# Attention ahead of two feed-forward layers: unscaled weights, sums carried along the row by TensorE, low halves on GpSimd, two more banks for scores

## The chip, the cores and the metric

The kernel runs on one core of one Trainium2 chip. The metric is device time in microseconds (us), the median of the runs shown. TensorE multiplies matrices (PE in the rows; PEld is its weight load), VectorE is DVE, ScalarE is ACT, GpSimd is POOL, and SyncE (SP) issues nearly all DMAs. Every engine works through its own list of instructions in order, so an instruction that waits holds up all that stand behind it on its engine.

## The reference, cut to what matters

```python
# q, k, v: (4, 12, 448, 64)
q_n, k_n = rmsnorm(q, g_q), rmsnorm(k, g_k)
scores = (q_n @ k_n.T) / sqrt(64)
scores = scores - max(scores, axis=-1)
attn = exp(scores)
attn = attn / (sum(attn, axis=-1) + 1e-9)
x = (attn @ v)                      # laid out as (1792, 768)
h = x @ w_in                        # 768 -> 2048
g = where(h > 0, h, exp(min(h, 0)) - 1)
x = g @ w_out                       # 2048 -> 768
# then: router x @ w_gate, greedy assignment of 1792 tokens to 8 experts
# (224 each), relu(x @ w1[e]) @ w2[e] on each expert's rows
```

The four lines from `scores` to `x`, and the low half of `g`, are what the change touches.

## The kernel before, in words

Numbers that need more than fp16 are kept as two fp16 halves, high and low, and a product takes three matmuls (high by high, low by high, high by low).

Attention walks over 4 batches of 6 pairs of heads. A pair has 448 query rows, in three blocks of 128 rows for both heads (`j` = 0 to 2) and one tail block (`j` = 3) in which the 64 last rows of both heads share a tile. For each block: `scores(j)` makes the products (six matmuls of 448 columns for two tiles `ps`), VectorE takes the row maximum (L533), ScalarE the exponential with its row sum (L535, `accum_out`). `weights(j)` adds 1e-9 (L540) and takes the reciprocal (L541) on VectorE, and GpSimd multiplies each row of the weights by it (L545; L543 also copies the tail rows of the second head to a place of their own). `turn_p(j)` transposes the scaled weights on TensorE (`pta`, `ptb`), and ScalarE (L559) and VectorE (L560) copy them to `PT`. After the four blocks `values` multiplies `PT` with v into `po`; ScalarE makes the high half of the result (L578), VectorE the low half (L579). Row sums lie along the partitions before the transposition; after it the query rows lie along the free dimension.

While batch b is in attention, the first feed-forward product of batch b-1 (`hidden`) runs between: 16 blocks f of 18 matmuls `ph`, then ScalarE and VectorE make `elu_g` (L682 to L685), ScalarE its high half `gt` (L687), VectorE the low half (L688), and SP stores both halves to DRAM (L689, L690). A ring of 6 buffers holds `gt`. The weights come in as pairs of 32-bit words that VectorE turns to fp32 in three instructions (L374, L377, L378), ScalarE scales and rounds them, GpSimd makes the low half (L382): `w_in` during batches 0 and 1, `w_out` during batches 1 and 2. There `w_out` is also transposed by DMA (`wt`) and multiplied with the gate (`gate_product`).

A table of steps (96 for a batch, 16 for a pair) sets what is written when: `scores(j)` at step 4j, `weights(j)` at 4j+1, `turn_p(j)` at 4j+5, `values` at 19, and the tile framework reorders instructions of an engine by its own simulated times. PSUM has 8 banks: 3 for scores (`psS`), 3 for transposes, values, gate and logits (`psT`), 2 for the first product (`psM`), which has nothing to do until batch 0 is through attention.

Stages by the trace, in us of the span: batch 0 from 27 to 140, batch 1 with the first product of batch 0 to 284, batch 2 to 422, batch 3 to 540, the first product of batch 3 to about 617. Then the second product with the routing, then the experts; the change touches nothing there.

## Time and profile before

| what | us |
|---|---|
| median of 3 runs (1158.93 to 1169.1) | 1161.26 |
| the profiled execution | 1164.11 |
| its span (first to last instruction) | 1162.4 |
| PE busy in the span | 1039.3 |
| DVE busy | 784.2 |
| ACT busy | 539.2 |
| POOL busy | 353.9 |

The share of busy time is an average over stages with different limits, so it is read by stage. A wait row names who waited for whom, with the total, the number of times and the longest. Mean durations of instructions on VectorE and GpSimd contain the time in which one held up the other.

### The profile page before, as it was taken

Reading aid. Unit: us, or ns where it says so; the run is one execution under the profiler, and the core shown is the slowest. Engines: PE = TensorE matmul, PEld = TensorE weight load, DVE = VectorE, ACT = ScalarE, POOL = GpSimd, SP = SyncE. Lnnn points to the kernel's source line nnn. Section 1 sums busy time; section 2 is a strip of 40 time slices with the busy share of each in tenths; the row PEclk is TensorE's granted clock in tenths of the full one; section 3 lists DMA queues with packets and bytes.
Section 4 is the critical chain, followed back from the end, with each engine's and each line's share of the span. In section 5 each row is a group of like instructions: output and inputs, shape, how many; then the busy total and the mean of one; then the engine's idle time right before and its main releaser. Section 6 shows DMA issues by size and latency. Waiting matters only on the chain.

```text
span 1162.4 us, 19353 instructions
## 1 busy us (share of the span) xinstructions
PE 1039.3 (89%) x7030; PEld 608.4 (52%) x7030; DVE 784.2 (67%) x1567; ACT 539.2 (46%) x1099; POOL 353.9 (30%) x462
## 2 busy tenths in 40 slices
PE   0687879897989999999999699999999898999997
PEld 0233334343444445444444345555546687888885
DVE  3788898999988775554337777877775565556520
ACT  2676677776777664554430410011102455555520
POOL 3687775757746451220000000000000412222100
PEclk9888889998999989999999899999999899999999
DMA  6355575569997825336823641030003778778710
GB/s 172 78 133 132 147 207 151 145 178 255 245 256 195 194 68 121 81 95 225 328 55 113 194 167 50 21 130 21 22 21 101 239 236 263 223 244 258 237 47 24
DMA packets 190319, 176.48 MB, mean 152 GB/s; under 512 B 114704, under 2 KB 161808, under 8 KB 189456
## 3 DMA queue, kind: packets, MB, share of 16 engines
q1 hardware_dynamic: 186064, 163.78, 49.5%
q0 software_dynamic: 3328, 11.01, 3.0%
q8 instruction: 55, 0.90, 0.3%
q10 hardware_dynamic: 832, 0.46, 0.1%
q14 instruction: 40, 0.33, 0.1%
HBM read 125.92 MB, written 31.98 MB: 136 GB/s over the span
## 4 chain that ended last, share of the span: by engine, by line
PE 48%; DVE 16%; DMA 13%; issue 10%; ACT 6%; POOL 4%; SPq 2%; POOLq 0%; DVEq 0%; ACTq 0%
PE py L324 17%; PE ph L324 12%; DMA st<-in_moe_w_dram 7%; PE po L324 4%; PE pye L324 3%; PE phe L324 3%; PE ps L324 3%; PE rt_pc L324 2%; DVE w L351 2%; DVE sm L533 2%; ACT w L350 2%; DVE cv L377 2%; PE pta L324 2%; DMA qn<-in_q_dram 2%; PE pl L324 1%
## 5 line engine op out<-in xcount | busy, mean ns | idle before, releaser
L324 PE MATMUL ph<-xT,w_in 128*128 128x448 f16 x1152 | 246.1, 358 | 8.2 <-DVE elu_g L685 5.2
L324 PE MATMUL py<-w_out,g 128*128 128x384 f16 x1152 | 204.5, 329 | 0.0
L324 PEld LDWEIGHTS <-w_in 128*128 128x128 f16 x1152 | 107.7, 99 | 127.7 <-issue 46.1
L351 DVE SCALAR_TENSOR_TENSOR w<-st,w 128x768 f16<-128x768 f32 (+1 forms) x112 | 119.2, 1072 | 76.7 <-ACT w L350 71.5
L545 POOL TENSOR_SCALAR pe<-pe,sm 128x448 f32<-128x448 f32 x168 | 126.7, 764 | 138.8 <-DVE sm L541 70.3
L324 PEld LDWEIGHTS <-g 128*128 128x128 f16 x1152 | 107.4, 98 | 89.3 <-issue 26.7
L324 PE MATMUL ps<-kT,qT 64*128 64x448 f16 (+1 forms) x576 | 97.0, 392 | 56.2 <-ACT pe L535 30.7
L350 ACT ACTIVATE w<-st 128x768 f16<-128x768 f32 (+1 forms) x112 | 103.6, 933 | 90.8 <-DMA st<-in_moe_w_dram 86.5
L535 ACT ACTIVATE pe<-ps,sm 128x448 f32<-128x448 f32 x168 | 105.9, 634 | 50.0 <-DVE sm L533 47.4
L324 PE MATMUL pye<-w,hT 128*112 128x512 f16 (+1 forms) x768 | 126.4, 326 | 0.0
L324 PEld LDWEIGHTS <-w 128*128 128x128 f16 x1152 | 111.8, 100 | 3.3 <-DVE xTe L917 1.2
L127 DVE TENSOR_SCALAR rt_C<-rt_row,rt_m 128x1792 f16<-128x1792 f32 x98 | 107.2, 1149 | 8.2 <-PE rt_pc L324 7.4
L324 PE MATMUL phe<-xTe,w 128*128 128x224 f16 x1080 | 111.4, 264 | 1.1 <-DVE xTe L917 1.1
L533 DVE TENSOR_REDUCE sm<-ps 128x1 f32<-128x448 f32 x168 | 100.2, 615 | 17.2 <-PE ps L324 15.2
L324 PEld LDWEIGHTS <-hT 128*112 128x112 f16 x768 | 91.6, 130 | 32.2
L815 ACT ACTIVATE xh<-py 128x384 f16<-128x384 f32 x28 | 13.7, 491 | 175.0 <-PE py L324 158.1
L324 PEld LDWEIGHTS <-qT 64*128 64x128 f16 (+1 forms) x576 | 27.7, 102 | 99.9 <-issue 66.7
L324 PE MATMUL pta<-id,pe 128*128 128x128 f32 x384 | 64.4, 289 | 15.1 <-POOL pe L545 5.8
L967 POOL DMA_INDIRECT out_dram<-yo,idx x16 | 19.5, 1220 | 179.6 <-DVE yo L966 178.0
L685 DVE SCALAR_TENSOR_TENSOR elu_g<-ph,elu_e 128x448 f32<-128x448 f32 x64 | 39.6, 619 | 48.3 <-ACT elu_e L683 48.1
L324 PEld LDWEIGHTS pta<-id,pe 128*128 128x128 f32 x384 | 45.2, 146 | 44.3 <-POOL pe L545 14.7
L201 POOL MEMSET rt_c<- 128x8 f16 x8 | 0.9, 123 | 220.7 <-DVE rt_c L207 216.6
(176 smaller groups left out, 1470.0 us busy)
## 6 DMA issues: line engine op xcount, KB each, us to landing
st<-in_moe_w_dram SPq DMA_DIRECT2D x48, 512.0 KB
st<-in_moe_w_dram SPq DMA_DIRECT2D x64, 384.0 KB
st<-in_moe_w_in_dram SPq DMA_DIRECT2D x24, 512.0 KB
g_d<-gt SPq DMA_DIRECT2D x64, 192.0 KB
g<-g_d SPq DMA_DIRECT2D x16, 768.0 KB
st<-in_moe_w_out_dram SPq DMA_DIRECT2D x16, 512.0 KB
gl<-g_d SPq DMA_DIRECT2D x32, 192.0 KB
wo_d<-wo SPq DMA_DIRECT2D x16, 384.0 KB
```

The costliest lines, as they stand in the source:

```text
L127: i = DVE.tensor_scalar(C.rearrange("p c t -> p (c t)"), row, m[:, s:s + 1], None, op0=ALU.is_le)
L201: nc.gpsimd.memset(c[:, 0:1, :], 0.0)
L324: i = PE_mm(o, l, r, **kw)
L350: ACT.activation(hi, st, AF.Copy, scale=SW)
L351: DVE.scalar_tensor_tensor(lo, st, SW, hi, op0=ALU.mult, op1=ALU.subtract)
L377: DVE.scalar_tensor_tensor(cv, st[:, :, 1], -0x40000000, cv, op0=ALU.bitwise_and, op1=ALU.bitwise_or)
L533: i = DVE.tensor_reduce(out=st[:, 0, u:u + 1], in_=ps[u], axis=AX.X, op=ALU.max, negate=True)
L535: ACT.activation(p[:, u, :], ps[u], AF.Exp, bias=st[:, 0, u:u + 1], accum_out=st[:, 1, u:u + 1])
L545: POOL.tensor_scalar(p[:, u, :], p[:, u, :], st[:, 2, u:u + 1], 1.0, op0=ALU.mult, op1=ALU.mult)
L685: DVE.scalar_tensor_tensor(gf, ph, -SG / SH, e, op0=ALU.mult, op1=ALU.min)
L815: ACT.activation(xh[:, 0], py, AF.Copy, scale=-SX2 / (SG * SW))
L967: st = POOL.indirect_dma_start(out=out, out_offset=bass.IndirectOffsetOnAxis(ap=idx[:, 1, 2 * e + hh:2 * e + hh + 1], axis=0), in_=yo, in_ ...
```

## The change

The weights are no longer scaled. `weights` is gone; a new `tail` keeps only the copy of the tail rows (GpSimd, 64 columns). The sums of all seven tiles of a pair stand in one tile `st`, and a new `sums`, written at step 15, makes all seven reciprocals (with the scale of the result in them) by one addition and one reciprocal on VectorE, splits them into two fp16 halves by two small GpSimd instructions, and has TensorE multiply the halves, broadcast over 64 columns, with the identity: 16 small matmuls bring the reciprocals from the partitions to the free dimension, in a bank of `psT`. ScalarE copies that to `x32`. `values` then multiplies `po` by it on VectorE, ScalarE rounds the high half, VectorE subtracts for the low half.

In `hidden` the low half of `gt` moves from VectorE to GpSimd. For the first five pairs, two of each five score tiles are in the banks `psM`. Some buffers are cut to make room: `ln`, `y2`, `wgt` to one, `wt` from three to two.

```diff
+        def bank(s):
+            s.nb = getattr(s, "nb", 0) + 1
+            if s.n < NP - 1 and s.nb % 5 in (1, 3):
+                return psM.tile([P, S], F32, tag="pm", name="psm")
+            return psS.tile([P, S], F32, tag="ps", name="ps")
...
-        def weights(s, j):
-            p, st = s.P[j]
-            w = 2 if j < NJ else 1
-            DVE.tensor_scalar(st[:, 2, 0:w], st[:, 1, 0:w], 1e-9, None, op0=ALU.add)
-            DVE.reciprocal(st[:, 2, 0:w], st[:, 2, 0:w])
-            if j == NJ:
-                POOL.tensor_scalar(p[:, 1, 0:TAIL], p[:, 0, MAIN:], st[:, 2, 0:1], 1.0, op0=ALU.mult, op1=ALU.mult)
-            for u in range(w):
-                POOL.tensor_scalar(p[:, u, :], p[:, u, :], st[:, 2, u:u + 1], 1.0, op0=ALU.mult, op1=ALU.mult)
+        def tail(s):
+            p = s.P[NJ]
+            POOL.tensor_scalar(p[:, 1, 0:TAIL], p[:, 0, MAIN:], 1.0, 1.0, op0=ALU.mult, op1=ALU.mult)
...
+        def sums(s):
+            iv = s.st[:, 2]
+            DVE.tensor_scalar(iv, s.st[:, 1], 1e-9, 1.0 / SX, op0=ALU.add, op1=ALU.mult)
+            DVE.reciprocal(iv, iv)
+            i16 = att.tile([P, 2, 2 * NJ + 1], F16, name="i16")
+            POOL.tensor_scalar(i16[:, 0], iv, 1.0, 1.0, op0=ALU.mult, op1=ALU.mult)
+            POOL.tensor_sub(i16[:, 1], iv, i16[:, 0])
+            pr = psT.tile([P, S], F32, tag="pt", name="pr")
+            kk = key()
+            for j in range(NJ + 1):
+                for z in range(2):
+                    for u in range(2):
...
+                        mm(pr[r, j * P:min(S, (j + 1) * P)], l, i, key=kk, start=(z == 0), stop=(z == 1),
+                           skip_group_check=True)
+            s.x = att.tile([P, S], F32, name="x32", bufs=1)
+            ACT.copy(s.x, pr)
...
-            ACT.activation(hi, po, AF.Copy, scale=SX)
-            DVE.scalar_tensor_tensor(lo, po, SX, hi, op0=ALU.mult, op1=ALU.subtract)
+            DVE.tensor_mul(s.x, po, s.x)
+            ACT.copy(hi, s.x)
+            DVE.tensor_sub(lo, s.x, hi)
...
-            DVE.tensor_sub(gt[:, 1], gf, gt[:, 0])
+            POOL.tensor_sub(gt[:, 1], gf, gt[:, 0])
...
-                    at(t + 4 * j + 1, p.weights, j)
                     at(t + 4 * j + 5, p.turn_p, j)
+                at(t + 4 * NJ + 1, p.tail)
+                at(t + 4 * NJ + 3, p.sums)
```

VectorE early in batch 1, where the first product begins; before (`sm` are the row statistics, `h` the halves of q and k, `cv` the converted weights, `gt` the halves of the first product):

```order
L378 SCALAR_TENSOR_TENSOR cv<-st,cv 128x512
L540 TENSOR_SCALAR sm<-sm 128x2
L541 RECIPROCAL sm<-sm 128x2
L481 TENSOR_TENSOR h_1815<-kn,h_1815 128x896
L374 TENSOR_SCALAR cv<-st 128x512
L688 TENSOR_TENSOR gt<-elu_g,gt 128x448
L377 SCALAR_TENSOR_TENSOR cv<-st,cv 128x512
L540 TENSOR_SCALAR sm<-sm 128x2
```

and of the change, at about the same place (`x` is the pair's result, `xT` its halves):

```order
L603 TENSOR_TENSOR x_1400<-po,x_1400 128x448
L378 SCALAR_TENSOR_TENSOR cv<-st,cv 128x512
L377 SCALAR_TENSOR_TENSOR cv<-st,cv 128x512
L564 COPY PT<-ptb 128x3x128
L574 TENSOR_SCALAR sm<-sm 128x7
L452 TENSOR_REDUCE ss<-sq 128x14
L378 SCALAR_TENSOR_TENSOR cv<-st,cv 128x512
L575 RECIPROCAL sm<-sm 128x7
L605 TENSOR_TENSOR xT<-x_1400,xT 128x448
```

The pairs of small instructions for each block are now one pair for each two heads, with other work between its two; `gt` is gone from VectorE, and the low half of the pair's result has become a multiplication and a subtraction.

GpSimd in the same stretch, before (`pe` are the weights, `w_in` the low half of the weights):

```order
L474 TENSOR_TENSOR qn<-qn,rs 128x896
L545 TENSOR_SCALAR pe<-pe,sm 128x448
L382 TENSOR_TENSOR w_in_133<-cv,w_in_133 128x512 x2
L545 TENSOR_SCALAR pe<-pe,sm 128x448 x4
L382 TENSOR_TENSOR w_in_133<-cv,w_in_133 128x512 x2
L494 TENSOR_SCALAR kT<-kT 128x2x64 x2
L545 TENSOR_SCALAR pe<-pe,sm 128x448 x2
```

and of the change (`i` are the halves of the reciprocals):

```order
L714 TENSOR_TENSOR gt<-elu_g,gt 128x448
L494 TENSOR_SCALAR kT<-kT 128x2x64 x2
L549 TENSOR_SCALAR pe<-pe 128x64
L454 TENSOR_TENSOR qn<-qn,gain 128x896
L382 TENSOR_TENSOR w_in_133<-cv,w_in_133 128x512
L714 TENSOR_TENSOR gt<-elu_g,gt 128x448
L577 TENSOR_SCALAR i_1641<-sm 128x7
L382 TENSOR_TENSOR w_in_134<-cv,w_in_134 128x512
L578 TENSOR_TENSOR i_1641<-sm,i_1641 128x7
```

The scalings of `pe` are gone, `gt` has come, and the two small instructions on the reciprocals stand among the long ones. On TensorE, in a pair of batch 1, the end of the new matmuls `pr` (16 with a weight load each) stands ahead of the pair's last transposition:

```order
L324 LDWEIGHTS i_1380
L324 MATMUL pr<-id_60,i_1380 64x64
L324 MATMUL pta<-id_65,pe 128x128 x4
L324 LDWEIGHTS w_in_133
L324 MATMUL ph<-xT,w_in_133 128x448
```

So TensorE, which takes its list in order, comes to `pr` before it can transpose the tail block or go on with the first product.

## Rows read from the trace of the kernel before

**Rows 1.** Busy time by engine, granted clock, DMA share and GB/s, by stage.

```profile
27.00:140.00 113.00, 85.58 (x443) 37.89 (x441) 93.37 (x186) 74.31 (x179) 81.52 (x101) 0.86 0.49 119
140.00:284.00 144.00, 122.93 (x712) 57.99 (x710) 133.38 (x259) 107.11 (x245) 99.66 (x115) 0.95 0.71 186
284.00:422.00 138.00, 124.96 (x809) 62.70 (x805) 118.09 (x290) 97.75 (x241) 79.65 (x101) 0.94 0.80 199
422.00:540.00 118.00, 118.00 (x719) 56.85 (x719) 68.16 (x167) 65.12 (x154) 25.86 (x42) 1.00 0.43 103
540.00:617.00 77.00, 75.47 (x401) 36.04 (x399) 23.49 (x43) 28.45 (x50) 3.47 (x24) 1.00 0.58 212
```

**Rows 2.** Waits in batch 0: who for whom, us in total, times, longest.

```profile
PE ps L324 <- ACT pe L535: 14.9, 15, 2.8
PEld pta L324 <- POOL pe L545: 11.1, 11, 3.8
DVE ss L452 <- ACT sq L451: 8.4, 6, 2.2
```

**Rows 3.** VectorE, addition to the sums (L540), by stage: stretch, us, busy (times).

```profile
27.00:140.00 113.00, 10.99 (x28) 0.86 0.49 119
140.00:284.00 144.00, 5.49 (x24) 0.95 0.71 186
284.00:422.00 138.00, 6.00 (x24) 0.94 0.80 199
```

**Rows 4.** VectorE, reciprocals (L541), by stage.

```profile
27.00:140.00 113.00, 4.00 (x26) 0.86 0.49 119
140.00:284.00 144.00, 3.96 (x26) 0.95 0.71 186
284.00:422.00 138.00, 3.70 (x24) 0.94 0.80 199
```

**Rows 5.** VectorE, low half of the first product (L688), by stage.

```profile
140.00:284.00 144.00, 13.05 (x16) 0.95 0.71 186
284.00:422.00 138.00, 12.16 (x16) 0.94 0.80 199
422.00:540.00 118.00, 10.38 (x16) 1.00 0.43 103
```

**Rows 6.** L688 alone: ns minimum/median/maximum, first and last start.

```profile
L688 DVE TENSOR_TENSOR gt<-elu_g,gt x64: 598/624/2060, 152.0 to 611.4; 128x448 f16<-128x448 f32 x64
```

**Rows 7.** Groups by line and shape: busy us, mean ns | idle before, what ended it.

```profile
L545 POOL TENSOR_SCALAR pe<-pe,sm 128x448 f32<-128x448 f32 x168 | 126.7, 764 | 138.8 <-DVE sm L541 70.3 <-PE pta L324 18.5 <-ACT cv L380 8.0
L382 POOL TENSOR_TENSOR w_in<-cv,w_in 128x512 f16<-128x512 f32 x24 | 31.2, 1302 | 7.3 <-ACT w_in L381 7.1
L382 POOL TENSOR_TENSOR wo<-cv,wo 128x256 f16<-128x256 f32 x16 | 14.0, 874 | 5.9 <-ACT wo L381 5.9
L465 POOL TENSOR_SCALAR ss<-ss 128x28 f32<-128x28 f32 x12 | 3.4, 286 | 9.5 <-ACT ln L459 9.1
L468 POOL TENSOR_TENSOR y<-y,ss 128x28 f32<-128x28 f32 x12 | 4.6, 383 | 0.6
L541 DVE RECIPROCAL sm<-sm 128x2 f32<-128x2 f32 x72 | 11.4, 159 | 1.0
L579 DVE SCALAR_TENSOR_TENSOR xT<-po,xT 128x448 f16<-128x448 f32 x24 | 14.8, 615 | 11.5 <-ACT xT L578 11.5
L578 ACT ACTIVATE xT<-po 128x448 f16<-128x448 f32 x24 | 12.9, 538 | 15.7 <-PE po L324 15.7
L324 PE MATMUL pte<-id,xg 112*128 112x112 f16 x192 | 14.5, 220 | 9.6 <-DMA xg<-x_d,idx 5.7 <-ACT xTe L917 3.0 <-issue 0.9
L324 PE MATMUL po<-PT,vn 128*64 128x448 f32 x288 | 63.2, 576 | 0.0
L324 PE MATMUL po<-PT,vt 128*128 128x448 f32 x48 | 27.0, 648 | 5.4 <-DVE PT L565 5.3
```

**Rows 8.** The chain that ended last, in batch 2: start, us, what.

```profile
334.39 5.05 DMA wt<-wo
359.09 3.75 DMA wt<-wo
```

More of the change, by code (lines that the diff above doesn't have):

```diff
@@ L456, in rms @@
         def rms(s):
-            ln = att.tile([P, 2, NB2], F32, name="ln")
+            ln = att.tile([P, 2, NB2], F32, name="ln", bufs=1)
             ACT.activation(ln, s.ss, AF.Ln, scale=1.0 / D, bias=eps)
@@ L465, in newton @@
             POOL.tensor_scalar(ss, ss, 1.0 / D, 1e-6, op0=ALU.mult, op1=ALU.add)
-            y2 = att.tile([P, 2, NB2], F32, name="y2")
+            y2 = att.tile([P, 2, NB2], F32, name="y2", bufs=1)
             POOL.tensor_mul(y2, rs, rs)
@@ L509, in scores @@
                 s.PT = att.tile([P, 2 * NJ + 1, S], F32, name="PT")
+                s.st = att.tile([P, 3, 2 * NJ + 1], F32, name="sm")
             w = 2 if j < NJ else 1
@@ L512, in scores @@
             s.P = getattr(s, "P", {})
-            st = att.tile([P, 3, 2], F32, name="sm", bufs=6)
-            s.P[j] = (p, st)
-            ps = [psS.tile([P, S], F32, tag="ps", name="ps") for u in range(w)]
+            st = s.st[:, :, 2 * j:2 * j + w]
+            s.P[j] = p
+            ps = [s.bank() for u in range(w)]
             kk = key()
@@ L535, in scores @@
                 ACT.activation(p[:, u, :], ps[u], AF.Exp, bias=st[:, 0, u:u + 1], accum_out=st[:, 1, u:u + 1])
-        def weights(s, j):
-            p, st = s.P[j]
-            w = 2 if j < NJ else 1
-            DVE.tensor_scalar(st[:, 2, 0:w], st[:, 1, 0:w], 1e-9, None, op0=ALU.add)
-            DVE.reciprocal(st[:, 2, 0:w], st[:, 2, 0:w])
-            if j == NJ:
-                POOL.tensor_scalar(p[:, 1, 0:TAIL], p[:, 0, MAIN:], st[:, 2, 0:1], 1.0, op0=ALU.mult, op1=ALU.mult)
-            for u in range(w):
-                POOL.tensor_scalar(p[:, u, :], p[:, u, :], st[:, 2, u:u + 1], 1.0, op0=ALU.mult, op1=ALU.mult)
+        def tail(s):
+            p = s.P[NJ]
+            POOL.tensor_scalar(p[:, 1, 0:TAIL], p[:, 0, MAIN:], 1.0, 1.0, op0=ALU.mult, op1=ALU.mult)
         def turn_p(s, j):
-            p = s.P.pop(j)[0].rearrange("p u k -> p (u k)")
+            p = s.P.pop(j).rearrange("p u k -> p (u k)")
             ta = psT.tile([P, NJ + 1, P], F32, tag="pt", name="pta")
@@ L565, in turn_p @@
                 DVE.tensor_copy(s.PT[TAIL:, NJ, MAIN:S], ta[TAIL:, NJ, TAIL:])
+        def sums(s):
[10 more added lines that the diff above has]
+                    for u in range(2):
+                        r = slice(u * D, (u + 1) * D)
+                        l, i = (i16[:, z, 2 * j + u:2 * j + u + 1].broadcast_to([P, D]), id16) if j < NJ else \
+                            (i16[r, z, 2 * j:2 * j + 1].broadcast_to([D, D]), id16[r, r])
+                        mm(pr[r, j * P:min(S, (j + 1) * P)], l, i, key=kk, start=(z == 0), stop=(z == 1),
+                           skip_group_check=True)
+            s.x = att.tile([P, S], F32, name="x32", bufs=1)
+            ACT.copy(s.x, pr)
         def values(s):
@@ L612, in gate_products @@
             for z in range(2):
-                wts.append(gat.tile([P, KC, P], F16, name="wt", bufs=3))
+                wts.append(gat.tile([P, KC, P], F16, name="wt"))
                 nc.sync.dma_start_transpose(wts[z], wo[:, z, :])
@@ L625, in gate_product @@
                    stop=(z == 1 and c == KC - 1), skip_group_check=True)
-        t = gat.tile([P, NE], F32, name="wgt")
+        t = gat.tile([P, NE], F32, name="wgt", bufs=1)
         ACT.copy(t, pw[:, NE:])
```

## The prediction

> **What bounds the kernel now.** I read the busy time by stage first, because the change touches only the five stages up to 617 us [rows 1]. In batch 3 (422 to 540) TensorE is busy for all 118.0 of 118 us, VectorE for 68.2: there TensorE is the bound, and time taken from VectorE buys nothing. In batches 1 and 2 VectorE is busy 133.4 of 144 and 118.1 of 138 us (93% and 86%), more than any other engine's useful work: the same attention and the same first product took TensorE 118 us in batch 3, so it could do batches 1 and 2 in about that. In batch 0 VectorE has 93.4 of 113 us, TensorE 85.6 with a mean granted clock of 0.86, that is, a part of the stage at 1.2 instead of 2.4 GHz after it had idled. GpSimd is busy for 81.5, 99.7 and 79.7 us in the first three, ScalarE for 74.3, 107.1 and 97.8: neither is the bound. So batches 0 to 2 go at VectorE's pace, with some latency in batch 0, and batch 3 and the first product of batch 3 (TensorE 75.5 of 77 us) at TensorE's.
>
> Second, the waits in batch 0 [rows 2]: TensorE waits 14.9 us for a bank of scores that ScalarE still reads, and 11.1 us (weight loads) for GpSimd's scaled weights. Third, the work that the change takes from VectorE, by stage [rows 3 to 5].
>
> **The change part by part.** All sums are for one stage of six pairs.
>
> *VectorE, sums.* Additions and reciprocals go: 10.99 + 4.00 = 15.0 us in batch 0, 5.49 + 3.96 = 9.5 in batch 1, 6.00 + 3.70 = 9.7 in batch 2 [rows 3, 4]. One addition and one reciprocal of 7 columns come for each pair. The nearest row is the reciprocal of 2 columns at 159 ns [rows 7]; 2 x 0.16 x 6 = 1.9 us.
>
> *VectorE, result.* Instead of one instruction on PSUM (L579, 615 ns [rows 7]) there are a multiplication that reads PSUM and SBUF, which I price like L579, so that it cancels, and a subtraction in SBUF with the shape of L688. That one takes 598 ns at least, 624 in the middle and up to 2060 [rows 6]; its mean by stage is 12.16/16 = 0.76 to 13.05/16 = 0.82 us beside a busy GpSimd and 10.38/16 = 0.65 in batch 3 [rows 5]. I take 0.72: 6 x 0.72 = 4.3 us (3.6 to 4.9).
>
> *VectorE, first product.* L688 goes: 13.05 us in batch 1, 12.16 in batch 2, 10.38 in batch 3 [rows 5].
>
> VectorE's balance is therefore -15.0 + 1.9 + 4.3 = -8.8 us in batch 0, -9.5 - 13.05 + 6.2 = -16.3 in batch 1, -9.7 - 12.16 + 6.2 = -15.7 in batch 2. Batch 3 and the 77 us behind it save on VectorE too, but TensorE hides that.
>
> *GpSimd.* 168 scalings at 764 ns go, 126.7 us in all [rows 7]. The low half of 448 columns has no row on GpSimd; between 874 ns for 256 and 1302 for 512 columns of the same operation [rows 7] it is 874 + 428 x 192/256 = 1195 ns, 1.2 us. 64 of them are 77 us, 19 in a stage. The two small instructions have 286 and 383 ns as their nearest rows [rows 7], 0.67 x 24 = 16 us. GpSimd is left with 126.7 - 77 - 16 = 34 us less work, and stays under 85 of about 128 us in batch 1. The subtraction takes 1.2 us where VectorE took 0.62, but the first product is 18 matmuls long and six buffers deep, so I cost that at nothing; the stores to DRAM and, from batch 2 on, the logits wait the half microsecond more. If the cover is gone, TensorE waits for a buffer.
>
> The Trainium skill speaks against this part: GPSIMD Engine Reference, section Engine selection, puts elementwise work on VectorE, since GpSimd is about twice as slow for two inputs. The trace agrees (1.2 against 0.62 us). By that rule alone the 64 moved instructions cost 64 x 0.6 = 37 us more than they did; that would be the sum if GpSimd were what everything waits for, and by the rows it isn't.
>
> *ScalarE.* A copy of 448 columns from PSUM for each pair, like L578 at 538 ns [rows 7]: 3.2 us a stage, 110 us in batch 1. That is under VectorE's new 117, but no longer far under.
>
> *TensorE.* 16 matmuls of 128 columns for each pair. The nearest row is the transposition of 112 columns, 192 of them busy for 14.5 us, 75 ns each [rows 7]: 1.2 us for a pair, 7.2 for a stage. The two heads write different halves of the partitions; where the value products do that, 288 of them take 63.2 us, 0.22 each, against 27.0/48 = 0.56 for the ones over all partitions [rows 7], so they run side by side, which would make it 3.6. I take 4 (nearer to the row that has the halves). In batches 0 to 2 this lies in TensorE's idle time (113 - 86, 144 - 123, 138 - 125 us [rows 1]); in batch 3 it adds 4 us.
>
> *TensorE's waits.* The transposition no longer waits for reciprocal and scaling; that is worth something in batch 0 (11.1 us [rows 2]), below nothing elsewhere. The chain now ends in `pr`, and behind `pr` stand the tail's transposition and the first product. Between the last scores of a pair and its `pr` the new order has work of the next pair or of the first product, so I take no wait.
>
> *Banks and buffers.* Two banks more in batch 0 answer the 14.9 us of waits for ScalarE [rows 2]; VectorE's row maxima are as many as before and end the same chain, so I count nothing beyond VectorE's saving, and 14.9 us as the far bound. The fewer buffers for `wt` cost nothing as long as the transposing DMAs come in time. They don't do so by much: in batch 2 the chain goes through them with pieces of 5.05 and 3.75 us [rows 8], with the DMA engines at 0.80 of the stage [rows 1]. 0.80 x 138 = 110 us of transfers would be 0.90 of a stage of 122 us. So of the 15.7 us in batch 2 I count 12.
>
> **Sum.** One microsecond of VectorE is one of the stage in batches 0 and 1: -8.8 - 16.3 - 12 + 4 = -33.1 us. The profiled execution took 1164.1 us (span 1162.4): 1131. The median of the runs is 2.85 us below it, so 1128.
>
> **The rivals.**
>
> *More comes back than VectorE saves.* If the waits were the bound, batch 0 would give 14.9 + 11.1 = 26 us, and batches 1 and 2 would fall to batch 3's 118 us, by 26 and 20: -26 - 26 - 20 + 4 = -68, so 1093. For it speaks that GpSimd leaves the chain from exponential to transposition; against it that VectorE would then have 117 us of work in 118.
>
> *The work hardly gets shorter.* ScalarE at 110 us, TensorE at 118 and DMA at 110 stand close behind VectorE, and in batch 0 VectorE also waits for ScalarE's squares (8.4 us [rows 2]). If only a third of VectorE's 41 us arrives, it is -14 + 4 = -10: 1151, no change by measure (I call within 1%, 1149.6 to 1172.9 us, the same).
>
> *Slower: TensorE waits at every `pr`.* The chain runs from the last row sum over VectorE's two instructions, between which the new order puts a reduction and a conversion, to GpSimd's two, between which stands a 1.3 us low half of the weights. If that comes 3.3 us late for each of 24 pairs, 24 x 3.3 = 79 us are lost, and 1128 + 79 = 1207. It decides from 33/24 = 1.4 us a pair on. For it speaks the order of the rows; against it that the transposition of the old kernel waited for the same chain, and lost 11 us to it in batch 0 only.
>
> *GpSimd holds VectorE up.* The Trainium skill, SBUF — State Buffer, section Who interferes with whom, says that a VectorE instruction with two inputs in SBUF is held by a GpSimd instruction that reads SBUF. The spread of L688 (598 to 2060 ns [rows 6]) agrees. As GpSimd's work falls by 34 us and VectorE loses 64 such instructions for 24 new ones, this leans to the faster side, and has no chance of its own.
>
> **How the numbers follow.** VectorE's saving, 0.50; more, 0.17; a third, 0.20; waits at `pr`, 0.13. The first has 1113 to 1145 as its own range: below it batch 0 with 11 us more and batch 2 with all of its 15.7, above it batches 1 and 2 with half of theirs and 7.2 us for TensorE in batch 3. To leave out 2 in 10, the range starts at 1093, the middle of the second case, holds the third and ends where a wait at `pr` of about 1.3 us for each pair would bring it, at 1160. Faster by over 1% are the first two and a quarter of the third, 0.72; slower a part of the last, 0.10; the same 0.18.
>
> **What would show it.** Batches 0 to 2 shorter by about 9, 16 and 12 us, batch 3 longer by about 4; VectorE's busy time in batch 1 near 117 us; 64 `gt` on GpSimd at about 1.2 us; `pr` matmuls at 75 ns or less with no wait of TensorE before them. It would be wrong if TensorE waits for the halves of the reciprocals, if stores of `gt` stand at the head of SP's list waiting for GpSimd while the loads behind them come late, or if batch 0 is held by its loads.

## The result, and the profile after

The changed kernel takes 1175.67 us (median of 4 runs, 1174.29 to 1178.95) where the kernel before, on the same chip, takes 1162.01: a ratio of 1.0113, 95% interval 1.0072 to 1.0155. It is slower by 1.1%; I had predicted 1128 us and a range up to 1160. The profiled execution has a span of 1173.2 us against 1162.4.

The busy time of the engines on the page after (us, share of the span, instructions):

```profile
PE 1051.0 (90%) x7414; PEld 617.5 (53%) x7414; DVE 748.9 (64%) x1383; ACT 548.6 (47%) x1123; POOL 306.9 (26%) x406
```

Over the whole span VectorE lost 784.2 - 748.9 = 35.3 us of work and GpSimd 353.9 - 306.9 = 47.0. So the change takes work away, and the time does not follow. Where it goes is seen by stage. The view is the same as [rows 1]: stretch, its length, busy time (instructions) of PE, PEld, DVE, ACT, POOL, granted clock, DMA share, GB/s. The bounds are the ends of batch 0 to 3 (the last low half of `xT` in each), then of the first product of batch 3:

```profile
27.00:150.30 123.30, 90.24 (x549) 42.37 (x548) 95.40 (x161) 81.03 (x192) 54.89 (x77) 0.86 0.47 115
150.30:283.60 133.30, 122.35 (x789) 59.14 (x787) 112.23 (x191) 101.20 (x236) 75.47 (x86) 0.99 0.74 184
283.60:431.50 147.90, 131.23 (x924) 65.40 (x924) 123.06 (x260) 105.17 (x259) 72.49 (x92) 0.97 0.82 198
431.50:551.30 119.80, 119.80 (x799) 57.81 (x798) 56.95 (x123) 66.22 (x157) 20.27 (x33) 1.00 0.40 98
551.30:629.00 77.70, 75.02 (x399) 35.96 (x397) 13.88 (x29) 29.17 (x50) 19.94 (x40) 1.00 0.57 212
```

By the same marks, to a tenth, the kernel before took 113.1, 143.8, 138.5, 117.0 and 77.7 us. So batch 0 is longer by 10.2 us, batch 1 shorter by 10.4, batch 2 longer by 9.3, batch 3 longer by 2.8, and what comes behind (routing and experts) shorter by 1.0: together +10.9 of the 10.8 us by which the span grew. Batches 0 and 1 taken together end at the same time as before (283.6 against 283.9).

VectorE's busy time against [rows 1] is 2.0 us more in batch 0, 21.2 less in batch 1 and 5.0 more in batch 2: 14.2 us less over the three, where I had forecast 40.8. A batch ends here with one instruction, and what else has been done by then is not the same in every kernel. Batch 0 holds 11 conversions of weights (L374) and 10 halves of q and k (L481), before the change 10 and 8; batch 1 holds 22 and 4, before 25 and 8. So a part of what batch 0 takes longer and batch 1 shorter is work that moved over the border between them, and the two are better read together.

The operations of the change, by line and shape (columns as in [rows 7]):

```profile
L714 POOL TENSOR_TENSOR gt<-elu_g,gt 128x448 f16<-128x448 f32 x64 | 71.8, 1122 | 163.2 <-ACT gt L713 162.5 <-ACT wgt L653 0.6
L324 PE MATMUL pr<-id,i 128*64 128x128 f16 x288 | 14.0, 231 | 2.4 <-ACT PT L563 1.2 <-POOL i L577 0.9 <-DVE PT L564 0.2
L603 DVE TENSOR_TENSOR x<-po,x 128x448 f32<-128x448 f32 x24 | 14.8, 618 | 30.3 <-PE po L324 30.3
L605 DVE TENSOR_TENSOR xT<-x,xT 128x448 f16<-128x448 f32 x24 | 19.0, 791 | 2.1 <-ACT xT L604 2.0
L590 ACT COPY x<-pr 128x448 f32<-128x448 f32 x24 | 12.7, 531 | 2.3 <-PE pr L324 2.2
L574 DVE TENSOR_SCALAR sm<-sm 128x7 f32<-128x7 f32 x24 | 8.1, 338 | 4.9 <-ACT pe L544 4.8
L575 DVE RECIPROCAL sm<-sm 128x7 f32<-128x7 f32 x24 | 4.7, 197 | 0.4
L324 PEld LDWEIGHTS <-i 128*64 128x64 f16 x288 | 9.7, 113 | 10.6 <-issue 7.0 <-POOL i L577 1.2 <-POOL i L578 1.1
```

The addition took twice its price (338 ns for 159), but no price here is far enough off to be worth more than 3 us a stage. TensorE's matmuls wait 2.4 us before `pr` in the whole span, of them 0.9 for GpSimd's halves, and the weight loads before them 2.3 for the halves: the rival "waits at every `pr`" did not come.

The waits in batch 0 of the kernel after (who for whom, us in total, times, longest), beside [rows 2]:

```profile
PE po L324 <- DVE PT L569: 10.4, 4, 4.3
ACT sq L451 <- DMA kn<-in_k_dram: 9.5, 3, 8.8
DVE ss L452 <- ACT sq L451: 9.4, 4, 5.9
PEld pta L324 <- ACT PT L563: 7.3, 5, 5.4
PE ps L324 <- ACT pe L544: 7.2, 5, 3.6
PEld pta L324 <- ACT pe L544: 5.4, 2, 5.0
```

The wait for a bank of scores has halved (14.9 to 7.2 us), and that of the transposition for GpSimd's scaled weights is gone. In their place the transposition waits for ScalarE, and the values for the copies of the last transposes. ScalarE's wait for the loads of k, 3.8 us in the kernel before, does not explain batch 0, though loads were one of my signs of being wrong: it is 9.6 us in a_noscale_wt3 (below), whose batch 0 takes 113.3 us.

The transposed gate weights, first before, then after: what TensorE idled for before the instructions that read `wt`, and who waited, with us and times (from the view of the tile `wt` between 240 and 440 us, that is, the end of batch 1 and batch 2). Before:

```profile
  DMA wt<-wo: 1.5, 2
  PEld L324: 0.8, 1
  PE pw L324: 0.7, 1
```

After:

```profile
  DMA wt<-wo: 24.0, 24
  PEld L324: 13.3, 12
  PE pw L324: 10.8, 12
```

With two buffers TensorE comes to `wt` too early 12 times and stands for 10.8 us, 8.2 of them in batch 2 (the weight loads count the same waits once more).

### The profile page after: what moved, and what is told of

It is laid out like the page before. It is cut to its first block, busy times and chain, and to the rows that moved or that the text cites. A ratio compares the mean times of both kernels' runs of the same rounds, so it can differ in the third digit from the quotient of the medians.

```text
span 1173.2 us, 19770 instructions
## 1 busy us (share of the span) xinstructions
PE 1051.0 (90%) x7414; PEld 617.5 (53%) x7414; DVE 748.9 (64%) x1383; ACT 548.6 (47%) x1123; POOL 306.9 (26%) x406
## 4 chain that ended last, share of the span: by engine, by line
PE 48%; DVE 16%; DMA 13%; issue 10%; ACT 6%; POOL 3%; SPq 3%; POOLq 0%; DVEq 0%; ACTq 0%
PE py L324 17%; PE ph L324 12%; DMA st<-in_moe_w_dram 8%; PE po L324 3%; PE ps L324 3%; PE pye L324 3%; DVE sm L542 2%; PE rt_pc L324 2%; DVE w L351 2%; PE pta L324 2%; ACT w L350 2%; DVE cv L377 2%; DMA wt<-wo 1%; PE phe L324 1%; PE pl L324 1%
## 5 line engine op out<-in xcount | busy, mean ns | idle before, releaser
L324 PE MATMUL ph<-xT,w_in 128*128 128x448 f16 x1152 | 240.8, 355 | 6.1 <-DVE elu_g L711 4.3
L324 PEld LDWEIGHTS <-w_in 128*128 128x128 f16 x1152 | 106.8, 98 | 119.8 <-issue 35.5
L324 PE MATMUL ps<-kT,qT 64*128 64x448 f16 (+1 forms) x531 | 90.7, 373 | 39.6 <-DMA qT<-h 24.9
L714 POOL TENSOR_TENSOR gt<-elu_g,gt 128x448 f16<-128x448 f32 x64 | 71.8, 1122 | 163.2 <-ACT gt L713 162.5
L544 ACT ACTIVATE pe<-ps,sm 128x448 f32<-128x448 f32 x153 | 96.3, 632 | 31.5 <-DVE sm L542 31.0
L542 DVE TENSOR_REDUCE sm<-ps 128x1 f32<-128x448 f32 x153 | 91.8, 615 | 11.9 <-PE ps L324 5.6
L324 PEld LDWEIGHTS <-qT 64*128 64x128 f16 (+1 forms) x576 | 26.3, 100 | 79.8 <-issue 46.8
L324 PE MATMUL po<-PT,vn 128*64 128x448 f32 x288 | 65.8, 596 | 0.0
```

The source lines that it names most:

```text
L324: i = PE_mm(o, l, r, **kw)
L542: i = DVE.tensor_reduce(out=st[:, 0, u:u + 1], in_=ps[u], axis=AX.X, op=ALU.max, negate=True)
L544: ACT.activation(p[:, u, :], ps[u], AF.Exp, bias=st[:, 0, u:u + 1], accum_out=st[:, 1, u:u + 1])
L714: POOL.tensor_sub(gt[:, 1], gf, gt[:, 0])
```

## The theories, and the lengths by stage

My first theory after the result was: batch 2 is longer because of two `wt` buffers instead of three, and batch 0 because `pr` and its chain stand in the way of something. The rivals: GpSimd's `gt` slows batch 2; VectorE's multiplication and subtraction at the end of each pair slow batch 0; the order that the framework makes by its simulated times is another after any edit, and the stages differ for that alone. The lengths by stage of all kernels that were run, from one profile each (us, batch 0 counted from 27 us), with the ratio of the times and its interval:

| kernel | b0 | b1 | b0 + b1 | b2 | b3 | ratio to before |
|---|---|---|---|---|---|---|
| before | 113.1 | 143.8 | 256.9 | 138.5 | 117.0 | 1 |
| b_wt2 | 112.5 | 142.7 | 255.2 | 149.8 | 116.8 | 1.0094 (1.0065 to 1.0123) |
| b_gate284 | 115.8 | 143.4 | 259.2 | 149.3 | 116.1 | 1.0112 (1.0069 to 1.0155) |
| b_gtpool | 115.1 | 141.0 | 256.1 | 156.6 | 117.0 | 1.0105 (1.0072 to 1.0139) |
| b_gate325 | 113.1 | 140.0 | 253.1 | 137.7 | 123.6 | 0.9971 (0.9954 to 0.9989) |
| b_gtbankgate | 115.8 | 143.5 | 259.3 | 137.3 | 123.6 | 0.999 (0.9968 to 1.0013) |
| after | 123.3 | 133.4 | 256.7 | 147.8 | 119.8 | 1.0113 (1.0072 to 1.0155) |
| a_gtdve | 122.0 | 136.1 | 258.1 | 150.3 | 120.5 | 1.0125 (1.0066 to 1.0184) |
| a_mulpool | 121.3 | 135.8 | 257.1 | 151.2 | 119.7 | 1.0125 (1.0065 to 1.0186) |
| a_nobank | 127.2 | 135.5 | 262.7 | 150.3 | 119.8 | 1.0188 (1.012 to 1.0256) |
| a_wt3cv2 | 123.5 | 136.4 | 259.9 | 149.1 | 119.8 | 1.0101 (1.0058 to 1.0144) |
| a_cv2x2 | 120.8 | 139.2 | 260.0 | 144.6 | 119.8 | 1.009 (1.0066 to 1.0115) |
| a_noscale_wt3 | 113.3 | 128.6 | 241.9 | 155.5 | 117.5 | 0.997 (0.9948 to 0.9992) |
| a_smallonly | 115.7 | 136.8 | 252.5 | 145.7 | 117.3 | 1.0024 (0.9994 to 1.0055) |
| a_sumsnocopy | 121.7 | 127.1 | 248.8 | 150.6 | 123.1 | 1.0028 (1.0004 to 1.0052) |
| a_sumsonly | 125.9 | 135.1 | 261.0 | 145.3 | 124.5 | 1.0104 (1.0065 to 1.0143) |
| a_prpm | 116.6 | 149.7 | 266.3 | 151.4 | 119.8 | 1.0208 (1.0168 to 1.0249) |
| a_prpm0 | 117.0 | 146.9 | 263.9 | 144.8 | 119.8 | 1.0164 (1.0139 to 1.019) |
| a_wt3cv2_gate | 121.4 | 136.0 | 257.4 | 136.5 | 124.3 | 1.004 (1.0013 to 1.0067) |
| a_prpm0_gate | 115.9 | 144.2 | 260.1 | 137.7 | 126.8 | 1.0071 (1.0043 to 1.0099) |

Names with b_ are the kernel before with an edit, with a_ the changed kernel with an edit.

How much a length means can be read from the traces. In before, b_wt2, b_gate284, b_gate325 and b_gtpool every engine has the same instructions in the same order until batch 0 is over, and it took 112.5 to 115.8 us: 3.3 us come without any edit. Nor is the profiled execution always a middle one: that of a_sumsnocopy took 1176.29 us where the median of its runs is 1169.56, those of a_noscale_wt3 and b_gtpool took 4.6 and 4.4 us more than their medians, and that of a_prpm0 6.3 less. The ratios are of the medians.

## Batch 2: the buffers of wt, or the order

**Two buffers alone.**

```diff
-wts.append(gat.tile([P, KC, P], F16, name="wt", bufs=3))
+wts.append(gat.tile([P, KC, P], F16, name="wt"))
```

> The kernel before with one thing of the change alone: two buffers for the transposed w_out (wt) instead of three. Theory 'buffer': the 9 us that batch 2 lost (147.9 against 138.5 us) are TensorE's waits for wt (18 us on its two lists after, 1.5 before), so this alone makes batch 2 longer by 6 to 10 us and the whole 1168 to 1172. Rival 'DMA share': batch 2 is held by the transfers as such, which are the same in both kernels, and the buffer moves nothing: 1162 within 4.

Measured: batch 2 took 149.8 us, 11.3 more than before, and no other batch moved by over 1.1 us. That looked like the whole answer. But TensorE waits for `wt` only 4.4 us there, not 11. In the same view of `wt`, of b_wt2:

```profile
  DMA wt<-wo: 9.8, 12
  PEld L324: 5.4, 6
  PE pw L324: 4.4, 6
```

**Three buffers given back to the changed kernel** (with two instead of three for `cv`, since the memory does not hold both).

```diff
-wts.append(gat.tile([P, KC, P], F16, name="wt"))
+wts.append(gat.tile([P, KC, P], F16, name="wt", bufs=3))
 (and the tag cv: bufs=3 -> bufs=2)
```

> The changed kernel with three buffers for wt again; the room comes from the converted weights (cv), two buffers instead of three. Theory 'buffer': batch 2 falls from 147.8 to 136 to 140 us, and the whole to 1162 to 1167, if the fewer cv buffers cost nothing. Rival 'transfers': batch 2 stays at 146 or more, the whole at 1174 or more.

Batch 2 took 149.1 us: nothing came back, though TensorE's wait for `wt` fell from 10.8 to 4.7 us in the same view. So the third buffer, paid for with one of `cv`, does not bring batch 2 back. A kernel with two `cv` buffers, two for `x32` and still two `wt` took 144.6 there, less than the one with three. Its own question was whether the single buffer of `x32` holds batches 0 and 1; they took 260.0 us against 256.7, so no gain shows:

> The changed kernel with two buffers for x32 instead of one (room again from cv). Theory 'one x32': the copy of a pair's reciprocals waits until the pair before has its low half, and holds a bank of psT meanwhile; with two, batches 0 and 1 together fall by 6 to 15 us from 257, the whole to 1160 to 1170. Rival: that copy has time; within 4 us of the two batches, the whole 1172 to 1180 (batch 2 has still two buffers for wt).

**An edit that takes no work away and adds none.** The kernel before, with the gate's products spread over steps 180 to 284 instead of 280.

```diff
-Spread(gate_products(), NG, 180, 280)
+Spread(gate_products(), NG, 180, 284)
```

> The kernel before with the gate's products spread over steps 180 to 284 instead of 180 to 280, which is next to nothing by itself but moves instructions in the scheduler's order. If batch 2 of the kernel before (138.5 us, where all changed kernels with the old spread have 144 to 157) is a robust result of its three `wt` buffers: batch 2 137 to 140 us and total 1160 to 1165 us. If the order there is fragile and every edit moves it: batch 2 143 to 152 us and total 1167 to 1177 us.

It took 1179.06 us, a ratio of 1.0112 (1.0069 to 1.0155): the same loss as the whole change. Its batch 2 by stage:

```profile
286.30:435.50 149.20, 130.75 (x828) 64.29 (x826) 124.11 (x293) 99.73 (x247) 85.05 (x103) 0.92 0.79 185
```

It has three `wt` buffers, and the view of `wt` shows next to no wait:

```profile
  DMA wt<-wo: 0.5, 2
  PEld L324: 0.3, 1
  PE pw L324: 0.2, 1
```

So batch 2 grows by 10.8 us with three buffers, with the same work in the program, and with next to nothing waiting for `wt`. What differs first is the order that the framework makes: in the two traces every engine has the same instructions in the same order up to 258 us of the span, and behind that it has not. In the longer stage VectorE is then busy for 124.1 us instead of 118.1, GpSimd for 85.1 instead of 79.7, and TensorE's mean granted clock is 0.92 instead of 0.94 [rows 1]. The clock is not what a long batch 2 needs, since the changed kernel has 147.8 us at 0.97. Of the 15 other kernels with a spread to 280 or 284, all have 144 to 157 us in batch 2; the 138.5 of before, on which my sum stood, was the exception. Which instruction's place makes the 11 us I did not find, and it stays open. The single buffers of `ln`, `y2` and `wgt` were given back in no run.

**The gate's products spread further**, into batch 3, in the kernel before and in the changed one (with the three buffers).

```diff
-Spread(gate_products(), NG, 180, 280)
+Spread(gate_products(), NG, 180, 325)
```

> The kernel before with the gate products spread over steps 180 to 325 instead of 180 to 280. If they are what holds batch 2: batch 2 falls from 138.5 to 126 to 131 us, batch 3 rises by 3 to 6, the whole 1155 to 1161. If VectorE's work as such holds batch 2, the same, as VectorE's work moves with them; if neither, within 4 us of 1163.

> As a_wt3cv2, with the gate products (loads, conversion, transposing DMA) spread over steps 180 to 325 instead of 180 to 280, so that a third of them falls into batch 3, where TensorE is the bound and VectorE, ScalarE and the DMA engines have half of their time free. If transfers and conversions hold batch 2, batch 2 falls to 122 to 130 us and batch 3 rises by 0 to 6: the whole 1148 to 1158. Rival 'in-order lists': the work just makes batch 3 longer, and the whole stays within 5 us of a_wt3cv2.

Batch 2 took 137.7 and 136.5 us, and in two more kernels with this spread 137.3 and 137.7: not the 122 to 131 that I expected if the gate's products were what holds it. Batch 3, at TensorE's pace, pays 6.6 us in the kernel before and 4.5 in the changed one (against a_wt3cv2). That is the one setting in which batch 2 had the same length in every kernel tried, four of them. Batch 2 and batch 3 of b_gate325 by stage:

```profile
280.10:417.90 137.80, 124.87 (x780) 61.47 (x779) 119.58 (x272) 99.06 (x240) 81.75 (x101) 0.94 0.81 195
417.90:541.40 123.50, 122.97 (x778) 59.35 (x776) 74.20 (x196) 68.48 (x166) 30.54 (x46) 1.00 0.50 120
```

Under this spread the change (with three `wt` and two `cv`) can be weighed with batch 2 out of the way: 1.004 against 0.9971, that is, 0.7% slower, about 8 us. Those are the 8.3 us of batch 0 (121.4 against 113.1), less 4.0 in batch 1 and 1.2 in batch 2, plus 0.7 in batch 3 and 3.2 behind it: 7.0 us of span. Each of the two kernels is one order of several possible, so a part of this may be the order again.

## Batch 0: what the sums cost

**The whole scaling left out.** No additions, reciprocals, `pr` or multiplication; the values' result is not divided by the row sums. Three `wt` buffers.

```diff
-at(t + 4 * NJ + 3, p.sums)
 (sums removed; values as in the kernel before)
```

> The changed kernel with three buffers for wt and without the scaling by the reciprocals at all: no sums, no pr, no x32, the halves of the result as before the change (so its output lacks the division by the row sums). Theory 'new chain': what VectorE saved in batches 0 and 1 is eaten by the new chain (sums, pr, x32 in one buffer, the multiplication that waits for the values' product); without it batches 0 and 1 together fall from 257 to 228 to 240 us. Rival 'VectorE not the bound': the pairs go at the pace of in-order lists and latencies whatever VectorE has to do; 250 us or more for the two.

Batches 0 and 1 by stage:

```profile
27.00:140.30 113.30, 83.74 (x442) 38.15 (x439) 87.21 (x136) 76.88 (x185) 52.88 (x65) 0.86 0.55 124
140.30:268.90 128.60, 118.26 (x692) 56.79 (x690) 105.60 (x182) 98.00 (x231) 66.38 (x69) 1.00 0.75 187
```

Batch 0 has 113.3 us with VectorE at 87.2 us and GpSimd at 52.9, and had 113.1 with 93.4 and 81.5 [rows 1]: taking VectorE's and GpSimd's scaling away altogether gives nothing there. Batch 1 falls by 15.2, to 128.6, though VectorE's work falls by 27.8; there TensorE's 118.3 is then the most. Together the two take 241.9 us, just above the 228 to 240 of the theory 'new chain' and well under its rival's 250: VectorE has 33.9 us less to do than before, 15.0 of them arrive in the time, and the changed kernel with its chain takes 14.8 again (256.7). This is one kernel in one order, but more than the 4.0 us by which before, b_wt2 and b_gate284 differ over the two batches. In all it came to 0.997, since batch 2 took 17 us more.

**The parts of the sums, one after the other.** From the kernel without scaling to the changed one, each without dividing the result: first the small instructions alone; then the 16 matmuls of each pair; then ScalarE's copy.

```diff
 a_smallonly:  DVE and POOL instructions of sums; pr and ACT.copy(s.x, pr) left out
 a_sumsnocopy: and the 16 matmuls pr
 a_sumsonly:   and ACT.copy(s.x, pr)
```

> The changed kernel with a part of the sums alone: one addition and one reciprocal of 7 columns on VectorE and the two halves of the reciprocals on GpSimd for each pair. The 16 matmuls `pr` on TensorE and the copy of `pr` on ScalarE are left out, and the values' result is not divided by the row sums. Batch 0 (27 us to the end of the 6th low half of xT) took 113.3 us with no sums at all and 125.9 with sums, `pr` and copy. If the small instructions at the end of VectorE's and GpSimd's lists hold batch 0: 121 to 127 us. If `pr` or its copy does it: 112 to 116 us. Total 1163 to 1178 us.

> The same with the 16 matmuls `pr` of each pair, but without ScalarE's copy of them; the values' result is not divided by the row sums. If TensorE's matmuls or the bank that `pr` takes from the three that transpositions and values share hold batch 0: 121 to 127 us against 112 to 116 without them. If ScalarE's copy, which waits for `pr` and stands ahead of exponentials and squares in its list, holds it: 112 to 116 us here as without `pr`. Total 1163 to 1178 us.

> The changed kernel with sums, pr and the copy to x32 as they are, but the result not multiplied by x32 (halves made from the values' product as before the change, so the output lacks the division by the row sums). It splits the 10 us of batch 0 (123.3 with the whole chain, 113.3 without it). Theory 'multiplication': the cost is VectorE's multiplication, which waits for the values' product at the head of its list; batch 0 at 112 to 116, batches 0 and 1 together 240 to 248. Theory 'pr': the cost is pr in TensorE's list and in a bank of psT, with its copy on ScalarE; batch 0 at 119 to 124, the two 250 or more.

Batch 0 of a_smallonly by stage:

```profile
27.00:142.70 115.70, 83.11 (x447) 38.34 (x446) 89.19 (x150) 76.11 (x184) 55.61 (x77) 0.85 0.53 120
```

and of a_sumsnocopy:

```profile
27.00:148.70 121.70, 89.88 (x542) 41.09 (x538) 92.91 (x155) 77.43 (x186) 57.45 (x79) 0.85 0.51 125
```

Batch 0 took 113.3, 115.7, 121.7 and 125.9 us: there the largest step, 6.0 us, comes with the matmuls. But its border moves, and a_sumsnocopy was profiled in a long execution. Batches 0 and 1 together took 241.9, 252.5, 248.8 and 261.0 us. By the medians, on one chip, the last three kernels took 1167.43, 1169.56 and 1179.75 us: the matmuls are worth 2 us there, and 10 come with ScalarE's copy (ratios 1.0028 and 1.0104, with intervals apart). Even that is less than the 1.1% that another order made in b_gate284. So the new chain, with the order that comes with it, costs 14.8 us in the two batches, and which of its links costs them is open. The matmuls' busy time, at least, is small: in the changed kernel they are, by stage and for the tile `pr` alone (PE, then ACT):

```profile
27.00:150.30 123.30, 4.41 (x96) 3.23 (x6) 0.86 0.47 115
150.30:283.60 133.30, 4.22 (x96) 3.20 (x6) 0.99 0.74 184
```

TensorE has 123.3 - 90.2 = 33 us idle in batch 0, room enough for 4.4. The steps of 2.4 and 4.2 us beside it are no larger than what other edits move batch 0 by (112.5 to 115.8 in the kernels without `pr`, 120.8 to 125.9 in those with it in `psT` and with banks for the scores).

**Multiplication and subtraction moved off VectorE** (to GpSimd, by way of a copy on ScalarE):

```diff
-DVE.tensor_mul(s.x, po, s.x)
-DVE.tensor_sub(lo, s.x, hi)
+o = s.PT[:, 0, :]; ACT.copy(o, po)
+POOL.tensor_mul(s.x, o, s.x)
+POOL.tensor_sub(lo, s.x, hi)
```

> The changed kernel, but ScalarE takes the values' result out of PSUM, GpSimd multiplies it with the reciprocals and makes the low half, so that nothing of the result is left on VectorE. Theory 'result on VectorE': VectorE's waits for the product (8.5 us in batch 0) and two instructions of 0.6 us a pair go; batch 0 falls by 6 to 12 us, batch 1 by 2 to 5, the whole to 1155 to 1167. Rival 'banks' or 'loads': batch 0 stays at 120 or more and the whole within 4 us of 1176.

Batch 0 took 121.3 us, batch 1 135.8: VectorE's two instructions at the end of a pair are not what holds batch 0.

**The bank of `pr`.** `pr` takes one of the three banks of `psT` that the transposes and the values go round in. In the changed kernel it was put into one of the two banks of the first product: throughout, and in another kernel for the six pairs of batch 0 alone.

```diff
-pr = psT.tile([P, S], F32, tag="pt", name="pr")
+pr = psM.tile([P, S], F32, tag="pm", name="pr")     # a_prpm
+(the same if s.n < NP, else psT)                    # a_prpm0
```

> The changed kernel, complete, with `pr` in one of the two banks of the first product instead of one of the three that the transpositions, the values and the gate's product share. If it is the missing bank that costs batch 0 its 10 us: batch 0 113 to 117 us, total 1163 to 1169 us. If it is the work itself or its place in the lists: batch 0 121 to 126 us, and batch 1 and 2 longer by the first product's wait for banks, total 1174 to 1182 us.

> The changed kernel with `pr` in a bank of the first product for the six pairs of batch 0 alone, where the first product doesn't run yet; from batch 1 on it lies where the change put it. With `pr` there throughout, batch 0 came down from 123.3 to 116.6 us and batch 1 rose from 133.4 to 149.7. If the bank is what costs batch 0 most: batch 0 115 to 118 us, batch 1 132 to 137, batch 2 anywhere from 144 to 152 (the old spread of the gate's products), total 1166 to 1176 us. If batch 0 gained from another order and not from the bank: batch 0 121 to 126 us, total 1173 to 1183.

Batch 0 fell by 6.7 and 6.3 us, to 116.6 and 117.0, and by 5.5 in a third kernel with it (a_prpm0_gate against a_wt3cv2_gate), as I expected if the missing bank costs it. But the three kernels have one and the same order of instructions until batch 0 is over, and not that of the changed kernel, so they do not tell the bank from the order. And they have moved work out of batch 0. Batches 0 and 1 of a_prpm0 by stage:

```profile
27.00:144.00 117.00, 91.34 (x526) 42.66 (x523) 86.06 (x144) 75.71 (x180) 50.02 (x73) 0.84 0.49 114
144.00:290.90 146.90, 131.10 (x824) 62.19 (x822) 131.21 (x220) 111.97 (x258) 87.61 (x95) 0.97 0.72 180
```

Its batch 0 holds 8 conversions (L374) and 8 halves (L481) instead of 11 and 10; VectorE has 9.3 us less to do there than in the changed kernel, and 19.0 more in batch 1. The two batches together take 263.9 and 266.3 us instead of 256.7, and 260.1 instead of 257.4 in the third kernel. So it is not shown that the missing bank costs time on the whole. The wait of the values for copies of the transposes, 10.4 us in the changed kernel, is 2.7 in batch 0 of a_prpm0, but the transposition's wait for ScalarE's exponentials is 13.9 us there for 4.2:

```profile
PE po L324 <- DVE PT L569: 2.7, 2, 1.9
PE pta L324 <- ACT pe L544: 13.9, 10, 3.9
```

In a_mulpool, with `pr` in its old bank, the values wait 2.9 us, and batch 0 takes 121.3 all the same. The totals got worse, 1188.74 and 1184.77 us (1.0208 and 1.0164), where the bank was to bring them under 1169 and 1176. The first product of batch 0 now starts 14 us later. The row of its matmuls (minimum/median/maximum ns, first and last start in us), after and in a_prpm0:

```profile
L324 PE MATMUL ph<-xT,w_in x1152: 349/352/581, 117.5 to 620.3; 128*128 128x448 f16 x192
```

```profile
L324 PE MATMUL ph<-xT,w_in x1152: 349/352/581, 131.6 to 624.5; 128*128 128x448 f16 x192
```

and batch 1 takes 146.9 instead of 133.4. That the last pairs' `pr` hold the bank that the first product would begin in fits the change's own rule, which lends these banks to the scores of the first five pairs only; a `pr` placed by that rule was not tried, so this cause is argued, not shown.

**The banks for scores taken back.**

```diff
-if s.n < NP - 1 and s.nb % 5 in (1, 3):
+if False:
```

> The changed kernel with all score tiles in their three old banks. Theory 'banks': the two banks let scores run ahead in TensorE's list, so that the values and transpositions of the pair before come later; without them batch 0 falls from 123 to about 113 us and the whole to about 1165. Rival 'result on VectorE': the loss of batch 0 is VectorE's wait for the values' product and ScalarE's for squares, and the banks help a little: without them batch 0 is 2 to 8 us longer still, 1178 to 1184.

Batch 0 took 127.2 us, 3.9 more, and the two batches together 262.7 instead of 256.7: the side of the rival. By these lengths the two banks help; but the order is another here from 25 us on, and the interval of the ratio (1.012 to 1.0256) overlaps that of the change.

## GpSimd's low halves

```diff
-POOL.tensor_sub(gt[:, 1], gf, gt[:, 0])
+DVE.tensor_sub(gt[:, 1], gf, gt[:, 0])          # a_gtdve; b_gtpool is the opposite edit on before
```

> The changed kernel with the low half of the first product back on VectorE. If GpSimd's lateness is what costs (theory 'GpSimd'): 1165 or less. If VectorE is still the bound of batch 1 (theory 'VectorE'): batch 1 gets 8 to 12 us longer (133 to about 143), batch 2 by 0 to 5 because the transfers hold it, the whole 1184 to 1190.

> The kernel before with one thing of the change alone: the low half of the first product on GpSimd. Theory 'VectorE in batch 1 alone': batch 1 falls from 143.8 by 4 to 10 us, batch 2 by 0 to 4 since the gate products hold it; the whole 1150 to 1160. Rival 'GpSimd is late': in the old kernel GpSimd's scalings stand before the transposition, the low halves among them make them late, batches 1 and 2 stay or grow; the whole 1162 to 1170.

In the changed kernel the move is worth 2.7 us in batch 1 and 2.5 in batch 2, no more than the order alone moves, and the ratios (1.0125 against 1.0113) do not tell the two apart; its 1179.27 us lie between what the two theories expected. In the kernel before, where GpSimd still scales the weights, batch 2 became 18 us longer, and the 1180.21 us are above what either theory expected. Batches 1 and 2 of b_gtpool:

```profile
142.10:283.10 141.00, 121.63 (x694) 57.06 (x693) 120.61 (x226) 101.31 (x232) 107.05 (x119) 0.97 0.70 176
283.10:439.70 156.60, 131.19 (x832) 64.25 (x830) 129.94 (x291) 103.76 (x256) 106.18 (x130) 0.92 0.80 188
```

VectorE fell from 133.4 to 120.6 us in batch 1 and the stage by 2.8: a microsecond of VectorE was at best a fifth of one of the stage, and 2.8 us is no more than two profiles of one order differ by. Of the 18 us in batch 2, 11 would be what b_gate284 loses there by its order alone; the rest, with GpSimd at 106 us, I put down to the longer way through GpSimd (TensorE's weight loads wait 7.7 us for scaled weights in batch 2, 0.7 in the kernel before), without a run that shows it. The ratio, 1.0105, is no worse than b_gate284's 1.0112.

## A better version

Two kernels combined what had helped: the kernel before with the wider spread, the banks and `gt` on GpSimd, and the changed one with the wider spread, three `wt` and `pr` elsewhere in batch 0.

```diff
 b_gtbankgate: before + POOL.tensor_sub(gt[:, 1], ...) + bank() + Spread(..., 180, 325)
 a_prpm0_gate: a_wt3cv2_gate + pr in psM if s.n < NP
```

> A version built from the parts that helped, without the new chain and with three buffers for wt: the kernel before with the low half of the first product on GpSimd, the two banks for scores and the gate products to step 325. Theory 'in-order lists, gains add where a stage is held by them': batch 0 109 to 113, batch 1 134 to 140, batch 2 122 to 128, batch 3 120 to 124, the whole 1138 to 1152. Rival: gains don't add, 1155 or more.

> The same with three buffers for `wt` (two for `cv`, to make room) and the gate's products spread to step 325. Without the other bank that kernel took 121.4 + 136.0 + 136.5 + 124.3 us for the four batches and 1171.3 in all. If the bank is worth 6 us of batch 0: 115 to 118 us there and 1163 to 1167 in all, still no faster than the kernel before with the same spread (1163.6). If the bank is worth nothing: 1170 to 1173.

Neither beats the wider spread alone: 0.999 and 1.0071. In a_prpm0_gate batch 0 gains 5.5 us and batch 1 loses 8.2. The fastest kernel of all was b_gate325, the kernel before with 325 in place of 280: 0.9971 (0.9954 to 0.9989), 1163.64 us beside 1166.86 on that chip, 1.4% below the changed kernel by their ratios.

## Why the prediction was wrong, point by point

My sum had -33.1 us; the span grew by 10.8, so 43.9 us are to be explained. By stage: batch 0 was to be -8.8 and was +10.2 (19.0 us); batch 1 -16.3 and -10.4 (5.9); batch 2 -12 and +9.3 (21.3); batch 3 +4 and +2.8 (-1.2); the rest 0 and -1.0.

- **"One microsecond of VectorE is one of the stage in batches 0 and 1."** This step failed. I took it from busy shares (93.4 of 113 us in batch 0 [rows 1]), though VectorE's idle 20 us there stood beside a wait for ScalarE's squares [rows 2]. The runs: over the two batches VectorE's busy time fell by 19.1 us and the time by 0.2. With all scaling gone (and `gt` on GpSimd as in the change) VectorE has 33.9 us less and the time 15.0, and batch 0 stays at 113.3 us. That batch 1 alone came to -10.4 for -16.3 is in part work that batch 0 had already done.
- **"VectorE's balance"**, the -8.8, -16.3 and -15.7 us behind that step, was mis-sized: -40.8 us in three batches, measured -14.2. The rows named in the sum gave -33.0 (59.3 us went, 26.3 came). But L378 and L481, as many as before, took 10.5 us longer (38.9 to 45.8, 25.9 to 29.6), and the rest I cannot place.
- **"In batches 0 to 2 this lies in TensorE's idle time."** This step failed too. The time of `pr` (4 us a stage; 4.4 measured) and the wait before it were near, but what else the new chain does to a stage (ScalarE's copy, the multiplication behind it, the bank of `psT` that `pr` takes from the transposes and the values, the other order) I put at nothing. Against the kernel without it the chain costs 14.8 us in batches 0 and 1; which link does is open. The text names the three banks of `psT`; I should have asked who else goes round in them.
- **"The fewer buffers for `wt` cost nothing as long as the transposing DMAs come in time."** They do not come in time: TensorE waits 10.8 us for them, against 0.7. The condition was stated and fell. Yet a_wt3cv2 shows that the third buffer does not bring batch 2 back.
- **"So of the 15.7 us in batch 2 I count 12."** It was +9.3, and the largest miss. The term had the wrong footing: I read 138 us as the state of batch 2 from which savings are taken, and an edit of four steps puts the kernel before at 149.3. Against that the changed kernel's 147.8 is 1.5 us better, not 9.3 worse; the gain of VectorE that I counted does not show even so, and its busy time in the stage rose by 5.0. My range held no term for the order of instructions, which moved a stage here by 11 us.
- **Batch 3 +4:** +2.8, right in kind; 4.4 us of `pr` there, TensorE busy throughout.
- **Prices:** VectorE in batch 1 near 117 us, measured 112.2, since batch 0 had taken on work of it; GpSimd 34 us less work, measured 47.0; `gt` on GpSimd 1.195 us, measured 1.122; `pr` 75 ns or less for 16 matmuls of 128 columns a pair, measured 14.0/288 = 49 ns (12 of a pair's 16 have 128 columns, the others 64); the copy 538 ns, measured 531; the addition and the reciprocal 159 ns each, measured 338 and 197; the subtraction 0.72 us, measured 0.79 (6.8 us for six in batch 1, 3.7 in batch 0). None of these prices of single instructions is worth more than 3 us a stage.
- **Rivals:** "waits at every `pr`" is refuted (2.4 us in all before the matmuls), though it had the right side, by luck. "The work hardly gets shorter" comes nearest for batches 0 and 1 together, which are 0.2 us shorter; the reason it gave in batch 0, VectorE's wait for ScalarE's squares, is little changed, 9.4 us against 8.4 [rows 2]. None of my rivals had a bank or the order in it.
- **The Trainium skill, GPSIMD Engine Reference, section Engine selection**, puts elementwise work with two inputs on VectorE. The instruction's price agrees in direction (1122 ns on GpSimd against 696 on VectorE in a_gtdve, 1.6 times). What that does to the time is not shown: in the changed kernel nothing that can be told from noise, and in the kernel before, with GpSimd at 107 us a stage, no more than another order makes.

## What to carry to other kernels

Where a scheduler orders by simulated times, first make an edit that changes no work (here four steps of a spread): what it moves, 1.1% in this kernel, is the least that an experiment on that place can mean, and a fast stage of the tuned kernel may be the lucky one. Before two lengths of a stage are compared, count what each holds: here three conversions and two halves crossed the border of batch 0, and the 6 us that it gained came back in batch 1 and more. Test that an engine is a stage's bound by taking its work away, as a_noscale_wt3 does, before its microseconds are added up as gains; here less than half of them arrived.

## What was not expected

Batches 0 and 1 together ended within 279 to 290 us of the span in 16 of the 20 kernels of the table, whatever was won in one of them (after: +10.2, -10.4; a_prpm0_gate: +2.8, +0.4). Work that crosses the border between the two is a part of that. Only taking the whole scaling away (268.9) or the division and the copy of `pr` (275.8) brought it lower, and `pr` in the first product's banks higher (290.9 and 293.2). What sets this common end is not settled: VectorE is busy for 112 of 133 us in batch 1 after, TensorE for 122, and neither is full.

The subtraction L605, 607 ns at the least and 624 in the middle, takes 1.14 us in the mean in batch 1 and 0.61 in batch 0, where GpSimd has 75 and 55 us of work: the same spread as in [rows 6], and more than I took.
